# Fifteen small, unused loads queued behind the last weight piece of a decode kernel

## The chip, the cores and the metric

The kernel runs on one core of a Trainium2 chip. The metric is the device time of one execution in microseconds (us). Before the change the median of three runs is 1329.7 us, with 1329.65 the lowest and 1329.88 the highest. A core has a matrix engine (PE), a vector engine (DVE), a scalar engine (ACT), GpSimd (POOL) and SyncE (SP, which only issues transfers and handles semaphores). Each engine follows its own instruction list, and engines wait for each other by semaphores. Sixteen DMA engines move data between the chip's memory (HBM) and the core's on-chip memory (SBUF). A transfer is issued by one engine's instruction list, is cut into packets over the DMA engines, and raises a semaphore when it has landed.

## The reference

One decode step for two batch rows `x` of 1024 elements: a gated mix of cached attention (A) and a small gated-MLP mixer (B).

```python
g = _sigmoid((x * gate_w).sum(-1, keepdims=True))
# A: q = x @ wq, 32 heads of 128, cache of 16384 positions for each batch and head
scores = einsum("bhqd,bhkd->bhqk", q, k_cache) * (Dh ** -0.5)
a = einsum("bhqk,bhkd->bhqd", softmax(scores), v_cache) -> (B, 1, H*Dh) @ wo
# B: (shifts with a sequence of 1 leave zeros, so gelu(layernorm(x) @ w1) meets w2 as zero)
h  = _gelu(_layernorm(x) @ w1);  x1 = x + shifted(h) @ w2
b  = x1 + _gelu(_layernorm(x1) @ w3) @ w4
return g * a + (1 - g) * b
```

All tensors are bfloat16. The two caches hold 2 x 32 x 16384 x 128 elements each, 537 MB together, and they are read once.

## The kernel before

The 32 heads are worked in 16 pairs, and each pair has two batch rows, so there are 32 units. A unit needs one K tile and one V tile. Each is 128 partitions by 64 KB and is loaded by one transfer from SP (`load_k`, line 113, `load_v`, line 118). For a K tile DVE transposes it in pieces (line 435) and PE forms the scores (line 441), then comes the softmax (lines 459 to 489), and PE multiplies the probabilities with the V tile (`pv`, line 495). A hardware loop (`tc.For_i`, line 684) does a pair in each round, one odd and one even unit. In its last round a conditional block (`tc.If`, line 688) also does the last unit, `last_unit`.

All instructions are kept in the order in which they are written on each engine (`in_order`, line 668), so the written order is the order of each queue.

The end of the kernel, which the change touches, runs like this:

- `last_unit` issues seven weight pieces from SP, the list `TAIL` (line 550), through `load_tail` (line 565): all of `wo`, then `w4` in three pieces of 16, 9 and 3 rows per partition, then the remaining 5 rows of `w1` in three pieces of 2, 2 and 1. Each piece has a semaphore of its own, `tail0` to `tail6`. The first two go out as `pv(0)` frees their place, the other five after `pv(1)`. All seven stand in SP's hardware queue (q1 in the profile) in that order. `w1`'s last piece is 128 partitions by 2048 bytes.
- Behind `last_unit` the loop ends. There all engines meet in a barrier: each finishes what it has, signals, and goes on when POOL has seen all of them. In the profile this is at lines 684 and 724.
- Then `output` (line 643) turns the attention result (`turn_heads`, line 526), and PE adds the weight pieces one by one, each behind a wait on the piece's semaphore (line 652). Behind the last `w4` piece `write_out` (line 578) gathers the two result rows and stores them by one transfer from ACT on queue q10 (line 586), which raises the semaphore `stored`. Behind the last `w1` piece ACT applies a GELU to the hidden row (line 663). That row meets only zeros in the reference, but the kernel computes it.
- POOL writes a one-element tile `end_mark` (line 664) and waits for `stored` (line 666). That is POOL's last work before the barrier that ends the program, in which again all engines meet: each engine drains and signals, POOL collects the signals and lets them go.

At the start of the kernel there are three small transfers on SP's queue that the prediction uses: `x` (two rows of 2048 bytes, line 101) and `gate_w` (one row of 2048 bytes, line 102), between the first `w1` piece (line 98) and `wq` (line 91).

Of the kernel before, what the change touches and what calls it, by code (L numbers as in the profile page):

```python
# [11 lines left out]
BF16 = mybir.dt.bfloat16  # L12
# [11 lines left out]
def kernel(  # L24
# [15 lines left out]
    nc = tc.nc  # L40
    P = nc.NUM_PARTITIONS
# [24 lines left out]
    const = ctx.enter_context(tc.tile_pool(name="const", bufs=1))  # L66
# [7 lines left out]
    def misc_psum(shape, dtype=FP32):  # L74
        return mps.tile(shape, dtype, tag="misc", name="misc")
# [41 lines left out]
    def load_v(hp, b, cell=V_CELL):  # L117
        nc.sync.dma_start(out=region(cell, NJ * Dh), in_=cache_rows(A_v_cache, hp, b))
# [6 lines left out]
        out=ident_s[:], in0=ident_f[:], scalar1=-scale, scalar2=None, op0=ALU.mult  # L125
# [10 lines left out]
        out=mask4[:], in_=mask4[:], compare_op=ALU.is_ge, fill=0.0,  # L136
# [3 lines left out]
        out=mask4[:], in_=mask4[:], compare_op=ALU.is_ge, fill=0.0,  # L140
# [11 lines left out]
        out=lmat[:].rearrange("p (g h k) -> p g h k", h=2, k=4),  # L152
        in_=hm2[:].unsqueeze(1).unsqueeze(3).to_broadcast([P, P // 8, 2, 4]),
# [5 lines left out]
        out=lane[:],  # L159
        in_=ident_f[:].rearrange("p (c k) -> p k c", k=QP),  # L160
# [5 lines left out]
    for g in range(Q4):  # L166
        nc.vector.tensor_scalar(
            out=spread[:, g],
# [159 lines left out]
    for shift in (1, -1, 2, -2):  # L328
# [10 lines left out]
        out=x1_rows[:], in_=oacc[1][:, 0:G1], func=ACTF.Copy, scale=omg_row[:, 0:1]  # L339
# [21 lines left out]
    for k in range(2):  # L361
        wide = mlp.tile([P, 16, QP], FP32, tag="wide", name="wide")
        nc.scalar.activation(  # L363
            out=wide[:].rearrange("p (c e) i -> p c e i", e=2),
            in_=oacc[k][:].rearrange("p (c i e) -> p c e i", i=QP, e=2),
# [15 lines left out]
    for e in range(2):  # L381
        half = slice(e * HALF, (e + 1) * HALF)
        nc.vector.tensor_copy(
            out=qdu[half].rearrange("p u v -> p (u v)"),
            in_=qdps[half, e].rearrange("p k g n -> p (k g n)"),
# [27 lines left out]
    def begin_rows(into, saved):  # L413
        for g in range(Q4):
            nc.tensor.matmul(
                into[g][QP * g : QP * g + B, 0:G1],
                lhsT=ident_f[:, QP * g : QP * g + B],
                rhs=saved[:],
                start=True,
                stop=False,  # L420
                skip_group_check=True,
            )
# [29 lines left out]
    def score_first(hp, b):  # L452
        write_qw(hp, b)
        score_chunks(b, halves[1 - b], True, False)

    def score_second(b):
        score_chunks(b, halves[b], False, True)

    def softmax_a(b):
        S = S_tiles[b]  # L460
        st = ppool.tile([P, GT, QP], FP32, name="St")
        nc.vector.transpose(out=st[:].rearrange("p j r -> p (j r)"), in_=S[:])  # L462
        m = stat.tile([P, 1], FP32, name="m")
        nc.vector.tensor_reduce(out=m[:], in_=st[:, :, 0:NG], axis=AX.XY, op=ALU.max)  # L464
        Dm = ppool.tile([P, P], FP32, name="Dm")
        nc.scalar.activation(out=Dm[:], in_=ident_s[:], func=ACTF.Copy, scale=m[:, 0:1])  # L466
        st_tiles[b] = (st, Dm)

    def softmax_b(b):
        st, Dm = st_tiles.pop(b)  # L470
        R_ps = misc_psum([P, P])
        nc.tensor.matmul(R_ps[:], lhsT=ones_f[:], rhs=Dm[:], start=True, stop=True)  # L472
        nb = stat.tile([P, 1], FP32, name="nb")
        rs = stat.tile([P, 1], FP32, name="rs")
        parts = [slice(e * HALF, (e + 1) * HALF) for e in range(2)]
        for rows in parts:
            nc.vector.tensor_reduce(out=nb[rows], in_=R_ps[rows, rows], axis=AX.X, op=ALU.min)  # L477
        for e, rows in enumerate(parts):
            nc.scalar.activation(  # L479
                out=pts[b][rows, :, e, :].rearrange("p (m a) k -> p a k m", a=GT // 4),  # L480
                in_=st[rows, :, 0:NG].rearrange("p (a k) m -> p a k m", k=4),
                func=ACTF.Exp,
                bias=nb[rows],
                scale=scale,
                accum_out=rs[rows],
            )
        tot_ps = misc_psum([P, 1])
        nc.tensor.matmul(tot_ps[:], lhsT=lmat[:], rhs=rs[:], start=True, stop=True)  # L488
        nc.vector.reciprocal(out=rinvs[b][:], in_=tot_ps[:])  # L489

    def pv(b, cell=V_CELL):
        V = view(cell)
        for g in range(NJ // 4):
            q = g % Q4
            nc.tensor.matmul(  # L495
                oacc[b][QP * q : QP * q + 8, :],
                lhsT=pts[b][:, g].rearrange("p h k -> p (h k)"),
                rhs=V[:, 4 * g : 4 * g + 4, :].rearrange("p j d -> p (j d)"),
                start=(g < Q4),
                stop=(g >= NJ // 4 - Q4),  # L500
            )
# [4 lines left out]
    def pv_end(hp, b):  # L506
        osb = ppool.tile([P, 4 * Dh], FP32, name="osb")
        nc.scalar.activation(  # L508
            out=osb[:], in_=oacc[b][:], func=ACTF.Copy, scale=rinvs[b][:, 0:1]
        )  # L510
        ot = misc_psum([P, 2])
        for k in range(4):
            nc.tensor.matmul(  # L513
                ot[:], lhsT=osb[:, k * Dh : (k + 1) * Dh], rhs=lane[:, k : k + 5 : 4],
                start=(k == 0), stop=(k == 3),
            )
        nc.vector.tensor_scalar(  # L517
            out=o_all[:, b, bass.ds(2 * hp, 2)], in0=ot[:], scalar1=g_rep[:, b : b + 1],
            scalar2=None, op0=ALU.mult,
        )  # L520
# [5 lines left out]
    def turn_heads():  # L526
        apart = mlp.tile([P, B, H, Q4], BF16, name="apart")
        for b in range(B):
            nc.vector.tensor_tensor(
                out=apart[:, b],  # L530
                in0=o_all[:, b].unsqueeze(2).to_broadcast([P, H, Q4]),
                in1=mask4[:].unsqueeze(1).to_broadcast([P, H, Q4]),
                op=ALU.mult,
            )
        ps = misc_psum([P, B, QP])
        for b in range(B):
            nc.tensor.matmul(
                ps[:, b], lhsT=apart[:, b].rearrange("p h c -> p (h c)"), rhs=lane_b[:],
                start=True, stop=True,
            )  # L540
        t = mlp.tile([P, QP, B], BF16, name="o_turned")
        nc.vector.tensor_copy(out=t[:], in_=ps[:].rearrange("p b r -> p r b"))
        return t
# [17 lines left out]
    def tail_piece(k):  # L561
        group, cell, at, src, r, n = TAIL[k]
        return region(cell, n * D, at * D)

    def load_tail(k):
        group, cell, at, src, r, n = TAIL[k]
        dma = nc.sync.dma_start(out=tail_piece(k), in_=src[:, r * D : (r + n) * D])
        dma.then_inc(tail_sems[k], 16)
        tc.no_tile_sem_insts.add(dma.ins.name)
        tc.add_to_no_dep_group(group, dma.ins)  # L570


    end_mark = const.tile([1, 1], FP32, name="end_mark")
    stored = tc.alloc_semaphore("stored")
    out_row = mlp.tile([B, D], BF16, name="out_row")
# [51 lines left out]
    def last_unit(hp):  # L627
        V_LAST = 0
        score_first(hp, 1)
        load_v(hp, 1, V_LAST)  # L630
        score_second(1)
        softmax_a(1)
        pv(0)
        load_tail(0)
        load_tail(1)
        pv_end(hp, 0)
        softmax_b(1)
        pv(1, V_LAST)
        for k in range(2, len(TAIL)):
            load_tail(k)  # L640
        pv_end(hp, 1)

    def output():
        begin_rows(arows, x1_rows)
        o_turned = turn_heads()
        hidden = [oacc[0]] * Q4
        begin_rows(hidden, h_early)
        nc.scalar.activation(
            out=h_rows[0:1, 0:1], in_=o_turned[0:1, 0, 0:1], func=ACTF.Gelu_apprx_tanh
        )  # L650
        for k, (group, cell, at, src, r, n) in enumerate(TAIL):
            nc.tensor.wait_ge(tail_sems[k], 16)
            if src is wo_rows:
                add_rows(arows, o_turned, 0, tail_piece(k), False, group)
            elif src is w4_rows:
                mm = add_rows(arows, h2T, r, tail_piece(k), r + n == FC, group)
                if r + n == FC:
                    tc.declare_fence(mm.ins, group=group)
                    write_out()
            else:  # L660
                mm = add_rows(hidden, xn1T, r, tail_piece(k), r + n == KC, group)
                tc.declare_fence(mm.ins, group=group)
        nc.scalar.activation(out=h_rows[:], in_=oacc[0][:, 0:G1], func=ACTF.Gelu_apprx_tanh)  # L663
        mark = nc.gpsimd.memset(end_mark[:], 0.0)
        tc.declare_fence(mark.ins, group="stored")
        nc.gpsimd.wait_ge(stored, 16)

    def in_order():

# [59 lines left out]
```

## Time and profile before

| what | value |
|---|---|
| median of three runs | 1329.7 us |
| time of the profiled execution | 1329.7 us |
| its span, first to last instruction | 1327.7 us |
| TensorE clock granted, share of full speed | 0.782 |
| HBM rate over the span | 431 GB/s |
| busy: PE, DVE, ACT, POOL | 760.3, 647.6, 132.5, 12.1 us |
| packets on q1 (SP), q10 (ACT) | 10662, 148 |
| share of time of the 16 DMA engines: q1, q10 | 99.4%, 0.4% |

The time is 2.0 us longer than the span: what lies before the first and behind the last instruction. The DMA engines are busy for nearly the whole span, so the kernel as a whole goes at the rate of its loads. What happens once the last load has landed is a stretch of about 1.7 us by the last rows of the timeline, and it consists of PE's last matmuls, ACT's GELU, and the barrier.

Beside what each engine did, the trace records every DMA packet (start, duration, bytes, queue) and every increment of a semaphore (its time). A transfer's own increments come as 4-byte packets behind its data packets. A packet's record does not name its DMA engine, but on one DMA engine the next packet's record starts 3 to 4 ns before the end of the one in front, so that neighbours can be matched over a short stretch.

### The profile page before, as it was taken

Reading aid. Unit: us, or ns where it says so; the run is one execution under the profiler, and the core shown is the slowest. Engines: PE = TensorE matmul, PEld = TensorE weight load, DVE = VectorE, ACT = ScalarE, POOL = GpSimd, SP = SyncE. Lnnn points to the kernel's source line nnn. Section 1 sums busy time; section 2 is a strip of 40 time slices with the busy share of each in tenths; the row PEclk is TensorE's granted clock in tenths of the full one; section 3 lists DMA queues with packets and bytes.
Section 4 is the critical chain, followed back from the end, with each engine's and each line's share of the span. In section 5 each row is a group of like instructions: output and inputs, shape, how many; then the busy total and the mean of one; then the engine's idle time right before and its main releaser. Section 6 shows DMA issues by size and latency. Waiting matters only on the chain.

```text
span 1327.7 us, 12974 instructions
## 1 busy us (share of the span) xinstructions
PE 760.3 (57%) x4956; PEld 330.6 (25%) x4956; DVE 647.6 (49%) x507; ACT 132.5 (10%) x207; POOL 12.1 (1%) x48
## 2 busy tenths in 40 slices
PE   3465566655556665555666555566655556665554
PEld 1122222222222222222222222222222223222222
DVE  2554455554445555444555544455554445555420
ACT  0011110011111001111100111110011111101110
POOL 1000000000000000000000000000000000000000
PEclk9677888777788877778887777888777788877776
DMA  9999999999999999999999999999999999999998
GB/s 403 441 439 423 435 434 438 424 432 440 438 426 432 440 423 434 438 440 424 432 440 434 428 434 438 424 434 438 440 424 432 440 424 432 438 440 424 432 440 369
DMA packets 10820, 572.69 MB, mean 431 GB/s; under 512 B 1205, under 2 KB 1205, under 8 KB 1850
## 3 DMA queue, kind: packets, MB, share of 16 engines
q1 hardware_dynamic: 10662, 570.44, 99.4%
q10 hardware_dynamic: 148, 2.10, 0.4%
q8 instruction: 8, 0.13, 0.0%
q14 instruction: 2, 0.02, 0.0%
HBM read 572.53 MB, written 0.00 MB: 431 GB/s over the span
## 4 chain that ended last, share of the span: by engine, by line
DMA 61%; PE 11%; DVE 10%; issue 4%; ACT 0%; DVEq 0%; PEld 0%; SPq 0%; ACTq 0%
DMA mem<-in_A_k_cache_dram 59%; PE S L441 11%; DVE KT L435 10%; DMA mem<-in_B_w_dram 3%; PE oacc L495 0%; DVEq L435 0%; ACT pt L479 0%; PEld L495 0%; SPq L113 0%; PE misc L513 0%; PE oacc L402 0%; ACT osb L508 0%; PEld misc L488 0%; ACT h_rows L663 0%; PE misc L472 0%
## 5 line engine op out<-in xcount | busy, mean ns | idle before, releaser
L441 PE MATMUL S<-KT,qw 128*128 128x512 bf16 x2048 | 548.2, 418 | 363.2 <-DVE KT L435 362.8
L435 DVE STREAM_TRANSPOSE KT<-mem 128x2048 f32<-128x2048 f32 x256 | 570.7, 2282 | 270.9 <-DMA mem<-in_A_k_cache_dram 212.0
L441 PEld LDWEIGHTS <-qw 128*128 128x128 bf16 x2048 | 216.5, 106 | 686.8 <-issue 482.6
L495 PE MATMUL oacc<-mem,pt 128*8 128x512 bf16 x2048 | 118.2, 384 | 7.6 <-DMA mem<-in_A_v_cache_dram 7.6
L466 ACT ACTIVATE Dm<-ident_s,m 128x128 f32<-128x128 f32 x32 | 12.9, 402 | 978.5 <-PE oacc L495 941.4
L479 ACT ACTIVATE pt<-St,nb 64x256 bf16<-64x256 f32 x64 | 89.7, 1401 | 61.1 <-DVE nb L477 60.2
L517 DVE TENSOR_SCALAR o_all<-misc,g_rep 128x2 f32 (+1 forms) x32 | 7.0, 220 | 163.2 <-PE misc L513 163.2
L488 PE MATMUL misc<-rs,lmat 128*128 128x1 f32 x64 | 18.7, 362 | 107.9 <-ACT pt L479 61.3
L495 PEld LDWEIGHTS <-pt 128*8 128x8 bf16 x2048 | 47.3, 87 | 75.6 <-issue 23.8
L513 PE MATMUL misc<-lane,osb 128*128 128x2 f32 x256 | 33.4, 252 | 45.3 <-ACT osb L508 45.3
L489 DVE RECIPROCAL rinv<-misc 128x1 f32<-128x1 f32 x32 | 5.4, 169 | 108.5 <-PE misc L488 60.5
L462 DVE STREAM_TRANSPOSE St<-S 128x512 f32<-128x512 f32 x32 | 22.9, 717 | 66.4 <-PE L495 64.4
L513 PEld LDWEIGHTS misc<-lane,osb 128*128 128x128 f32 x256 | 31.1, 191 | 61.0 <-ACT osb L508 31.6
L488 PEld LDWEIGHTS misc<-rs,lmat 128*128 128x128 f32 x64 | 16.0, 311 | 114.8 <-ACT pt L479 65.3
L508 ACT ACTIVATE osb<-oacc,rinv 128x512 f32<-128x512 f32 x32 | 22.0, 687 | 88.3 <-PE oacc L495 88.3
L479 ACT ACTIVATION_READ_ACCUMULATOR pt<-St,nb 64x1 f32 x64 | 30.6, 477 | 0.0
L389 POOL TENSOR_TENSOR qw<-qdu,mask 128x16 bf16<-128x16 bf16 x32 | 7.3, 261 | 1161.6 <-PEq L688 1074.6
L477 DVE TENSOR_REDUCE nb<-misc 64x1 f32<-64x64 f32 x64 | 14.2, 222 | 7.0 <-PE misc L472 4.9
L472 PE MATMUL misc<-Dm,ones_f 128*128 128x128 f32 x64 | 16.6, 346 | 0.0
L464 DVE TENSOR_REDUCE m<-St 128x1 f32<-128x256 f32 x32 | 13.4, 420 | 1.1
L583 DVE CAST out_row<-arow 2x256 bf16<-2x256 f32 x1 | 0.4, 413 | 26.9 <-PE S L402 26.9
L217 DVE STREAM_TRANSPOSE turn<-wide 128x512 f32<-128x512 f32 (+2 forms) x4 | 3.0, 744 | 17.5 <-ACT wide L363 11.5
(104 smaller groups left out, 95.4 us busy)
## 6 DMA issues: line engine op xcount, KB each, us to landing
mem<-in_B_w_dram SPq DMA_DIRECT2D x1, 7168.0 KB, 31.6
mem<-in_B_w_dram SPq DMA_DIRECT2D x1, 4096.0 KB, 42.1
mem<-in_B_w_dram SPq DMA_DIRECT2D x1, 2304.0 KB, 32.2
mem<-in_B_w_dram ACTq DMA_DIRECT2D x1, 2048.0 KB, 11.8
mem<-in_B_w_dram SPq DMA_DIRECT2D x2, 768.0 KB, 21.1
mem<-in_B_w_dram SPq DMA_DIRECT2D x2, 512.0 KB, 33.9
mem<-in_A_k_cache_dram SPq DMA_DIRECT2D x32, 27.8
mem<-in_A_v_cache_dram SPq DMA_DIRECT2D x32, 32.4
```

Of the source, the lines that this page charges most:

```text
L435: nc.vector.transpose(out=kt[:], in_=Kc.rearrange("p j d -> p (j d)").bitcast(FP32))
L441: nc.tensor.matmul(S, lhsT=qw[b][:, v, NG - 1 - m : NG - 1 - m + P], rhs=ktb[:, half * GT : (half + 1) * GT, w, :, e], start=(first and n ...
L462: nc.vector.transpose(out=st[:].rearrange("p j r -> p (j r)"), in_=S[:])
L464: nc.vector.tensor_reduce(out=m[:], in_=st[:, :, 0:NG], axis=AX.XY, op=ALU.max)
L466: nc.scalar.activation(out=Dm[:], in_=ident_s[:], func=ACTF.Copy, scale=m[:, 0:1])
L472: nc.tensor.matmul(R_ps[:], lhsT=ones_f[:], rhs=Dm[:], start=True, stop=True)
L477: nc.vector.tensor_reduce(out=nb[rows], in_=R_ps[rows, rows], axis=AX.X, op=ALU.min)
L479: nc.scalar.activation(out=pts[b][rows, :, e, :].rearrange("p (m a) k -> p a k m", a=GT // 4), in_=st[rows, :, 0:NG].rearrange("p (a k) m ...
L488: nc.tensor.matmul(tot_ps[:], lhsT=lmat[:], rhs=rs[:], start=True, stop=True)
L495: nc.tensor.matmul(oacc[b][QP * q : QP * q + 8, :], lhsT=pts[b][:, g].rearrange("p h k -> p (h k)"), rhs=V[:, 4 * g : 4 * g + 4, :].rearra ...
L508: nc.scalar.activation(out=osb[:], in_=oacc[b][:], func=ACTF.Copy, scale=rinvs[b][:, 0:1])
L513: nc.tensor.matmul(ot[:], lhsT=osb[:, k * Dh : (k + 1) * Dh], rhs=lane[:, k : k + 5 : 4], start=(k == 0), stop=(k == 3),)
```

## The change

A tile `marks` of 16 partitions by 512 elements is added that nothing reads, and a semaphore `marked`. Behind the seven weight pieces, still in `last_unit`, SP issues fifteen transfers, number k from 1 to 15. Number k copies k rows of 8 x k bytes out of `wo` (from the first k of its 128 row groups, which lie 64 KB apart) to k partitions of `marks`. They write disjoint columns. All of them raise `marked`, by 16 each. At the end POOL waits for `marked` to reach 240 behind its wait for `stored`.

```diff
+    marks = const.tile([16, 512], BF16, name="marks")
+    marked = tc.alloc_semaphore("marked")
+    wo_flat = A_wo.rearrange("(p r) n -> p (r n)", p=P)
+    MARKS = range(1, 16)
+
+    def load_marks():
+        at = 0
+        for k in MARKS:
+            dma = nc.sync.dma_start(
+                out=marks[0:k, at : at + 4 * k], in_=wo_flat[0:k, 0 : 4 * k]
+            )
+            dma.then_inc(marked, 16)
+            tc.no_tile_sem_insts.add(dma.ins.name)
+            tc.add_to_no_dep_group("marked", dma.ins)
+            at += 4 * k
...
         for k in range(2, len(TAIL)):
             load_tail(k)
+        load_marks()
         pv_end(hp, 1)
...
         mark = nc.gpsimd.memset(end_mark[:], 0.0)
         tc.declare_fence(mark.ins, group="stored")
+        tc.declare_fence(mark.ins, group="marked")
         nc.gpsimd.wait_ge(stored, 16)
+        nc.gpsimd.wait_ge(marked, 16 * len(MARKS))
```

## The prediction

> **What bounds the kernel now.** I read the page first: its chain of work, then the waits of SP's queue, then the timeline of the last 55 us, and last the trace's records of packets and semaphore increments at both ends of the span. The page says that the loads bound the whole:
>
> ```profile
> PEclk9677888777788877778887777888777788877776
> DMA  9999999999999999999999999999999999999998
> ...
> DMA 61%; PE 11%; DVE 10%; issue 4%; ACT 0%; DVEq 0%; PEld 0%; SPq 0%; ACTq 0%
> ```
>
> The reader is to see that the DMA row is full in every slice. A transfer that stands in front of other loads costs its own time. The fifteen new ones stand behind all other loads of SP's queue, so what counts is who waits for them. First SP, which must issue them before the barrier at the loop's end; its waits near the end, in us (total, times, longest):
>
> ```profile
> SPq L724 <- DVE out_row L583: 28.6, 1, 28.6
> ...
> SPq L724 <- ACT h_rows L663: 2.2, 1, 2.2
> SPq L684 <- DVE o_all L517: 2.0, 1, 2.0
> ```
>
> SP arrives at the loop's end 2.0 us before DVE, and afterwards it stands for 28.6 and 2.2 us. Next the timeline (start, duration, what, and in brackets the idle time before it):
>
> ```profile
> 1288.85 3.10 SPq L567 DMA_DIRECT2D mem<-in_B_w_dram  x5
> ```
>
> ```profile
> 1295.84 0.09 POOL L664 MEMSET end_mark<- 1x1 f32 x1 [103.23 <-POOLq L724]
> ...
> 1297.13 0.20 ACT L648 ACTIVATE h_rows<-o_turned 1x1 bf16<-1x1 bf16 x1
> ...
> 1305.93 0.38 PE L402 MATMUL arow<-mem,o_turned 128*2 128x256 bf16 x2 [8.75 <-DMA mem<-in_A_wo_dram]
> ...
> 1324.71 0.53 ACTq L586 DMA_DIRECT2D out_dram<-out_row  x1
> 1325.43 0.10 PEld L402 LDWEIGHTS <-xn1T 128*2 128x2 bf16 x8 [1.12 <-DMA mem<-in_B_w_dram]
> 1325.43 1.01 PE L402 MATMUL oacc<-mem,xn1T 128*2 128x256 bf16 x12 [0.62 <-DMA mem<-in_B_w_dram]
> ...
> 1326.49 0.38 ACT L663 ACTIVATE h_rows<-oacc 128x256 bf16<-128x256 f32 x1 [1.92 <-PE oacc L402]
> ```
>
> SP's last issue is over at 1291.95. The barrier lets the engines go at 1295.8. The preparation of the output takes 1.5 us, and then PE stands 8.75 us until `wo` is there. At the end PE's last matmuls follow w1's last piece, whose increments arrive up to 1326.02, ACT is done at 1326.87, and SP's signal at 1327.02 is the last that POOL collects, at 1327.04. From there 0.71 us remain. So the present end goes w1, PE, ACT, SP, barrier. POOL is early: `stored` is full at 1325.96, POOL's drain is over at 1326.19, and it stands 0.85 us.
>
> **The change part by part.**
>
> *Issues on SP.* Fifteen instructions. The nearest rows are the small loads at the start:
>
> ```profile
> 1.25 0.33 SPq L101 DMA_DIRECT2D rows<-in_A_x_dram  x1
> ...
> 1.63 0.22 SPq L102 DMA_DIRECT2D rows<-in_gate_w_dram  x1
> ```
>
> With the 0.53 us of the store as the other end and some 0.045 us between two, fifteen take 4.0 to 8.6 us, near 5.5 us by the row with two rows. SP leaves them at 1296.0 to 1300.6. Its remaining steps to the barrier took 0.75 us before the wait and 0.5 us behind it, so the barrier opens at 1297.2 to 1301.9 where it opened at 1295.8. DVE, PE, ACT and POOL all wait for it. What they do there is 1.5 us of preparation in front of PE's 8.75 us wait for `wo`: the delay of 1.5 to 6.1 us is covered and costs nothing; the cover is gone at about 0.73 us for each issue. What is late next would be wo's matmuls, with further waits of 3.34 and 2.33 us behind them.
>
> *The data.* In all 8 x (1 + 4 + ... + 225) = 9920 bytes, at most 960 on one DMA engine, which by the 80 ns from one 2048-byte packet to the next is 0.04 us. They are behind w1 in the same queue, so w1, PE and ACT lose nothing. The result's two rows go by q10 and share DMA engines with them; see below.
>
> *The increments.* This is where I expect the cost. At the start x (two rows) made two data packets and two increments, and gate_w (one row) one of each. I read from that that k rows use k DMA engines (if they used fewer, the first would still get all fifteen). The gate packet began 6 ns behind the second increment packet of x, on the same DMA engine, so small transfers share their first engine: it gets fifteen increments, the next fourteen, and so on. On that engine three increments went out back to back: that of w2 (q10), of x and of gate_w, packets at 9.492, 9.498 and 9.584 us. They landed at 9.887, 10.069 and 10.251: 0.182 us apart each time, though the packets were 0.006 and 0.086 us apart. On x's other engine the pair landed at 9.742 and 9.924, again 0.182. So increments of one DMA engine take turns, also over two queues, and 2048 bytes of data between two of them add nothing. (Where they lie farther apart, as in w1's pieces, an increment lands some 0.44 us after its packet.)
>
> The sixteen increments of w1's last piece land between 1324.23 and 1326.02, nine of them from 1325.69 on. Which engine is the first of the small ones isn't recorded; only the store's two packets, at 1325.48 and 1325.52 on idle engines, say that its two engines were through w1 by then. An engine late in w1 among the first three gives 1325.85 plus 13 to 15 times 0.182, that is 1328.2 to 1328.6. Taking every order of the sixteen as equally likely (the first two done by 1325.92), the mean of the latest is 1328.3 and eight in ten lie between 1328.0 and 1328.6. The store's own increments join the same line on two of these engines, at most 0.18 more. I take 1328.4 for the last of `stored` and `marked`.
>
> *POOL.* It waits for `marked` with nothing behind but the drain and the final barrier, for which all engines wait. Increments that land by 1325.96 + 0.85 = 1326.81 would cost nothing. 1328.4 is 1.6 us later, which moves the end from the chain w1, PE, ACT, SP to the chain w1, increments, POOL. The second wait instruction is some tens of ns. One semaphore more and fifteen instructions more in a block that runs once I cost at nothing: in the loop SP waits 16 us at a time for DVE (509.5 us over 31 waits).
>
> *Bounds of a turn.* Nothing in the trace shows fifteen in a row, or packets of 8 to 120 bytes. Below: turns that overlap, 0. Above: each transfer begins only when the one before has landed, 0.44 us after its packet plus some 0.06, so 0.5 us; then the same average puts the last landing at 1332.8, +6.0 us. I take 0.182, since the three rows agree to the ns with and without data between.
>
> *The sum.* 0 (issues) + 0 (data) + 1.6 (increments and POOL) on a profiled execution of 1329.7 us, which is also the median: 1331.3 us, +0.12%. From no change this kernel's measurement tells about 0.2%, here 2.7 us.
>
> [...]
>
> **The rivals.**
>
> *A costlier turn (slower).* Place: the first DMA engine's line behind w1. Price: more than 0.182 us for each transfer. From 0.26 us on, the last landing is past 1329.5 and the kernel is over 0.2% slower. For it: 8-byte pieces have no row here, the trace has only three pairs, and each transfer's read could wait for the former's increment. Against it: x and gate_w, with separate transfers and data between. [...]
>
> *SP is held up (slower).* SP had at most seven transfers outstanding (at 1291.95), each issue still at 0.33 to 0.37 us. With 22 the queue might be full. SP would then issue the last ones only when w4 and w1 have drained, near 1322 to 1326, and the barrier and all of the output come behind: 1.4 us preparation, then PE's 6.3, 3.2, 1.6 and 0.8 us, then the store, about 2.2. That ends 12 to 15 us later: 1342 to 1345. No row speaks for it, none shows more than seven.
>
> *All hidden (same).* If increments overlap, `marked` is full by 1326.8, and the end stays with ACT: 1329.7. The 0.182 us speaks against it.
>
> *Faster.* Only a different spread of the last loads over the engines could do it; SP's order in front of the marks is unchanged. I see no row for more than some tenths.
>
> **How the numbers follow.** Turns of about 0.18 us, 1330.9 to 1332.3: 0.46. All hidden: 0.06. Costlier turn: 0.35. SP held up: 0.10. Faster: 0.03. Same is 0.46 + 0.06 = 0.52, slower 0.45, faster 0.03. The likeliest case alone says 1331.3. For eight in ten I leave out SP held up and the turns beyond 0.5 us (some 0.10), and start where all is hidden: 1329.6 to 1336.0.
>
> **What would show it.** After: SP's fifteen issues of 0.22 to 0.53 us from 1292 on; the barrier at 1297 to 1302 and PE's wait for `wo` shorter by the same, its wo matmuls still at about 1305.9; w1, PE and ACT at the end as before; the increments of `marked` on the fullest engine 0.18 us apart, the last near 1328.4; and a span of 1329.3. Wrong it would be by a turn that is not 0.18 us, by an SP issue that lasts microseconds, or by wo matmuls that begin late.

## The result, and the profile after

The changed kernel takes 1333.55 us in the median of eight runs (1332.29 to 1334.89). The kernel before takes 1329.82 in the eight runs beside it (1329.49 to 1329.97). The ratio is 1.003, with a 95% interval of 1.0019 to 1.0041: slower by 3.7 us, or 0.28%. The time lies in the predicted range (1329.6 to 1336.0), but it isn't the forecast of 1331.3, and it lies past the 0.2% that the prediction took as the line between slower and no change (the interval reaches down to 0.19%). The runs also spread over 2.6 us, where the kernel before spreads over 0.5.

The profiled execution took 1333.65 us, with a span of 1331.6. The waits of SP's queue and of the engines near the end, in the columns used before (total, times, longest, in us):

```profile
SPq L743 <- DVE out_row L599: 12.8, 1, 12.8
...
SPq L743 <- ACT h_rows L680: 1.0, 1, 1.0
```

```profile
PE S L415 <- PEq L743: 21.5, 1, 21.5
...
DVE out_row L599 <- PE S L402: 10.6, 1, 10.6
```

SP's 2.0 us wait for DVE at the loop's end is gone, and its long wait of 28.6 us has shrunk to 12.8. PE, on the other hand, stands 21.5 us at the barrier. The timeline says why (start, duration, what, idle time before it):

```profile
1292.05 22.84 SPq L581 DMA_DIRECT2D marks<-in_A_wo_dram  x15
...
1316.34 0.09 POOL L681 MEMSET end_mark<- 1x1 f32 x1 [124.38 <-POOLq L743]
...
1317.88 0.14 PEld L402 LDWEIGHTS <-o_turned 128*2 128x2 bf16 x4 [0.28 <-DVE o_turned L542]
...
1322.39 1.84 PEld L402 LDWEIGHTS <-o_turned 128*2 128x2 bf16 x71 [2.13 <-issue]
1324.24 1.61 PEld L402 LDWEIGHTS <-h2T 128*2 128x2 bf16 x57
1326.68 1.40 PEld L402 LDWEIGHTS <-h2T 128*2 128x2 bf16 x55 [0.82 <-issue]
1328.09 0.53 PEld L402 LDWEIGHTS <-xn1T 128*2 128x2 bf16 x20
...
1329.35 0.53 ACTq L602 DMA_DIRECT2D out_dram<-out_row  x1
1329.93 0.38 ACT L680 ACTIVATE h_rows<-oacc 128x256 bf16<-128x256 f32 x1 [0.72 <-DVE out_row L599]
```

The fifteen issues last 22.84 us, not 4.0 to 8.6. The first five take 0.24 to 0.29 us each. The sixth takes 2.61, the seventh 4.80, and the rest 1.18 to 2.38 each. So SP is done with its issues 22.9 us later, at 1314.89. It no longer waits for DVE, and the barrier opens 20.5 us later, at 1316.26 instead of 1295.76. By then `wo` has long landed. PE does all of its output work in one go, from 1317.88 on, and no row of it waits for a transfer any more: the two waits that are left inside it say "issue". The store goes out at 1329.35, 4.64 us later than before. POOL had 0.85 us to spare, and the difference, 3.8, is what the span grew by (from 1327.75 to 1331.59).

The increments did what was predicted of them: the last one for `marked` landed at 1328.04. But `stored` was full only at 1330.60, so they cost nothing here.

Before, the end of the kernel hung on the chain w1, PE, ACT, SP. Now it hangs on SP's issues, the barrier, PE, the store and POOL.

### The profile page after: what moved, and what is told of

It reads as the page before. It is cut to its first block, busy times and chain, and to the rows that moved or that the text cites. A ratio compares the mean times of both kernels' runs of the same rounds, so it can differ in the third digit from the quotient of the medians.

```text
span 1331.6 us, 12990 instructions
## 1 busy us (share of the span) xinstructions
PE 754.6 (57%) x4956; PEld 329.5 (25%) x4956; DVE 648.1 (49%) x507; ACT 132.5 (10%) x207; POOL 12.0 (1%) x48
## 5 line engine op out<-in xcount | busy, mean ns | idle before, releaser
L462 DVE STREAM_TRANSPOSE St<-S 128x512 f32<-128x512 f32 x32 | 22.9, 717 | 66.4 <-PE L495 64.4
L415 PE MATMUL S<-x_rows,ident_f 128*2 128x256 f32 x4 | 1.0, 608 | 21.5 <-PEq L743 21.5
L472 PEld LDWEIGHTS misc<-Dm,ones_f 128*128 128x128 f32 x64 | 11.0, 216 | 0.4 <-issue 0.4
## 6 DMA issues: line engine op xcount, KB each, us to landing
mem<-in_B_w_dram SPq DMA_DIRECT2D x2, 768.0 KB, 21.5
```

## The experiments

The theory after this reading: SP is held in its issues because too much stands in its queue, and the price is the late barrier. Rivals: the small transfers or their increments cost the time where they are.

### The transfers issued behind the barrier

```diff
         for k in range(2, len(TAIL)):
             load_tail(k)
-        load_marks()
         pv_end(hp, 1)
...
         o_turned = turn_heads()
+        nc.vector.memset(marks[:], 0.0)
+        load_marks()
```

> The fifteen transfers are issued behind the loop's barrier (at the start of the output, behind a memset of their tile), with everything else as in the changed kernel. Theory: SP held in its issues costs only because SP owes the barrier its signal; here it owes nobody anything until 1324, so the barrier opens near 1295.8 again, PE works through the pieces as they land, and only the increments are left: marked full near 1328.0 to 1328.6, 1330.9 to 1331.4 us, about 1.5 above the kernel before. Rival, the increments cost nothing (other work covers them): 1329.7. Rival, the transfers cost the 3.7 us by themselves wherever they are issued: 1333.5.

It took 1331.12 us (1330.84 to 1331.44), against 1329.88 (1329.55 to 1330.11) for the kernel before in these runs: ratio 1.001, interval 1.0000 to 1.0019. The interval reaches down to no change, but none of the ten runs overlaps with any of the 27. Its timeline:

```profile
1296.33 0.09 POOL L682 MEMSET end_mark<- 1x1 f32 x1 [103.17 <-POOLq L744]
...
1298.11 16.80 SPq L581 DMA_DIRECT2D marks<-in_A_wo_dram  x15
1306.14 4.63 PEld L402 LDWEIGHTS <-o_turned 128*2 128x2 bf16 x128 [8.55 <-issue]
...
1324.94 0.53 ACTq L602 DMA_DIRECT2D out_dram<-out_row  x1
...
1326.76 0.38 ACT L681 ACTIVATE h_rows<-oacc 128x256 bf16<-128x256 f32 x1 [1.96 <-PE oacc L402]
```

SP is held here too, 16.80 us for the fifteen, but it owes nobody a signal. The barrier is early, PE starts on `wo` when it lands, and the store goes out at 1324.94. The trace's semaphore records have the last increment of `marked` at 1328.00 and POOL going on at 1328.02, 0.74 us after the last of the other engines. So this kernel has the end that the prediction described, and its 1.24 us stand beside the predicted 1.6.

### A late barrier without the transfers

```diff
         for k in range(2, len(TAIL)):
             load_tail(k)
+        nc.sync.wait_ge(tail_sems[1], 16)
         pv_end(hp, 1)
```

> The kernel before, without any of the fifteen transfers, but SP waits for the landing of w4's first piece (near 1315.3) ahead of the loop's barrier. Theory (the late barrier is the cost): the barrier opens near 1316.2 as in the changed kernel, and the time is 1333.5 with a spread of some 2 us between runs. Rival (the small transfers or their increments are the cost): 1329.7.

It took 1334.22 us (1333.64 to 1334.68), ratio 1.0032, interval 1.0019 to 1.0044. The barrier opened at 1317.44, 1.2 us later than in the changed kernel:

```profile
1317.52 0.09 POOL L665 MEMSET end_mark<- 1x1 f32 x1 [124.96 <-POOLq L725]
...
1323.80 1.84 PEld L402 LDWEIGHTS <-o_turned 128*2 128x2 bf16 x71 [1.92 <-issue]
...
1329.96 0.53 ACTq L586 DMA_DIRECT2D out_dram<-out_row  x1
```

Not one small transfer is in this kernel, and it loses 4.3 us, with the same kind of stop inside PE's work. So a late barrier alone is enough for a loss of this size. The spread of 1 us is less than the 2 expected.

The second form of this edit waits for `tail_sems[0]`, that is for `wo`:

> The kernel before, but SP waits for the landing of wo (near 1305.8) ahead of the loop's barrier. Theory: the barrier opens near 1306.7, PE is ready near 1308.2, 2.3 us behind wo's landing, and its later waits for w4 (3.3 and 2.3 us) take that up: 1329.7 to 1330.0. Rival (any delay of the barrier beyond PE's 8.75 us wait is paid in full): 1332.

1329.89 us (1329.66 to 1330.23), ratio 1.0001, interval 0.9991 to 1.001. The barrier opened near 1307.5 and PE's output work began at 1309.15, 3.2 us later than before. Its later waits took that up, as the prediction said of delays beyond the 8.75 us. PE stopped for "issue" here too, for 1.86 and 2.54 us, and still came to a wait for weights behind that, so the stops cost nothing here.

### Five transfers instead of fifteen

```diff
-    MARKS = range(1, 16)
+    MARKS = range(1, 6)
```

> Only the transfers of 1 to 5 rows, in the place of the change. Theory (SP is held from the sixth on, since its queue is full): five issues of 0.24 to 0.29 us, the barrier near 1295.8 to 1296, marked full by 1326.9 at the latest, 1329.7 to 1329.9. Rival (each small transfer costs a fifteenth of the 3.7 us): 1331.0.

1329.95 us (1329.70 to 1330.21), ratio 1.0001, interval 0.9991 to 1.001. Five issues of 0.24 to 0.29 us, barrier at 1295.6. Five cost nothing that these runs can tell, so the loss is no fixed price for each transfer. At which number between five and fifteen it sets in, no run shows.

### The same fifteen on ACT's queue

```diff
-        load_marks()
         pv_end(hp, 1)
+        load_marks()
...
-            dma = nc.sync.dma_start(
+            dma = nc.scalar.dma_start(
                 out=marks[0:k, at : at + 4 * k], in_=wo_flat[0:k, 0 : 4 * k]
```

> The same fifteen transfers, issued by ACT behind its last activation of the loop (near 1293.8), so on queue q10, which is empty then; the rest as in the changed kernel. Theory (SP's own queue is full, and that holds SP): ACT isn't held, fifteen issues of 0.25 to 0.55 us are over by 1298 to 1302, the barrier opens by 1303, within PE's wait for wo, and the transfers land long before the end, among the loads: 1329.7 to 1330.0. Rival (what is full is shared by both queues): ACT is held instead of SP, the barrier opens near 1316, 1333.5.

1329.85 us (1329.77 to 1330.25), ratio 1.0002, interval 0.9992 to 1.0011. Each issue took 0.24 to 0.50 us, at the same time at which SP would have been held, and the barrier opened at 1299.6:

```profile
1293.23 5.54 ACTq L581 DMA_DIRECT2D marks<-in_A_wo_dram  x15
```

So what holds SP belongs to SP's queue, and is not something that both queues share. The same 9920 bytes and 120 increments cost nothing when they don't stand behind the last weights.

### What fills the queue

Four kernels ask whether packets or transfers count, and on what. Each was run once. The first replaces the fifteen by one transfer of 16 rows with 30 pieces of 8 bytes each:

```diff
-        for k in MARKS:
-            dma = nc.sync.dma_start(
-                out=marks[0:k, at : at + 4 * k], in_=wo_flat[0:k, 0 : 4 * k]
-            )
+        dma = nc.sync.dma_start(
+            out=marks[:, 0 : 30 * 8].rearrange("p (j e) -> p j e", e=8)[:, :, 0:4],
+            in_=wo_flat[0:16, 0 : 30 * 8].rearrange("p (j e) -> p j e", e=8)[:, :, 0:4],
+        )
```

> One transfer in the place of the fifteen: 16 rows, each of 30 pieces of 8 bytes, so that each DMA engine gets 30 data packets and one increment, as many packets as the fullest engine has in the change, but one transfer and one turn. If packets for each DMA engine fill the queue: this single issue lasts some 20 us, the barrier opens at 1313 to 1316, and the time is near 1333. If the number of transfers outstanding fills it (twelve went out freely): one issue of 0.3 us, barrier at 1295.8, 1329.7.

It took 1330.03 us beside 1329.67. Its issue took 0.42 us. Taken alone this speaks for transfers and against packets.

The second gives all fifteen one row:

```diff
-                out=marks[0:k, at : at + 4 * k], in_=wo_flat[0:k, 0 : 4 * k]
+                out=marks[0:1, at : at + 4 * k], in_=wo_flat[0:1, 0 : 4 * k]
```

> Fifteen transfers in the place of the change, each of one row (8 to 120 bytes), so all on one DMA engine: 15 data packets and 15 increments there, none on the others. If what fills is counted for each DMA engine or in transfers: SP is held as in the change, from about the sixth on, barrier near 1316, 1333.5. If it is the sum over the engines (240 packets in the change, 30 here): no hold, barrier near 1297, and only the turns are left, 1330.5 to 1331.4.

It took 1333.23 us beside 1329.67. SP's row in the timeline:

```profile
1292.08 22.85 SPq L581 DMA_DIRECT2D marks<-in_A_wo_dram  x15
```

22.85 us against 22.84 in the change, and the sixth is again the first to be held. One DMA engine's share is enough; the sum over the engines (30 packets instead of 240) isn't what counts. In this run the fifteen increments stand alone on their engine, and the trace has them landing from 1324.669 to 1327.214 us, each 0.18 us behind the one before (2.545 us over 14 steps, single steps of 0.180 to 0.186): the predicted turn, with packets of 8 to 120 bytes.

The third joins w1's last three pieces, which takes two transfers and 18 packets for each engine out of the queue:

```diff
-        ("hidden0", 1, 0, w1_rows, W1_EARLY, 2),
-        ("hidden1", 1, 2, w1_rows, W1_EARLY + 2, 2),
-        ("hidden2", 1, 4, w1_rows, W1_EARLY + 4, 1),
+        ("hidden0", 1, 0, w1_rows, W1_EARLY, 5),
```

> The changed kernel with the three last pieces of w1 as one transfer of five rows, so two transfers and 18 packets for each DMA engine fewer stand ahead of the small ones. If the number of transfers is what SP's queue can take (twelve went out freely, the thirteenth was held): the first seven small ones go out freely and the eighth is held. If it is packets for each DMA engine: some nine more, so nearly all fifteen go out freely. If neither counts but only the time or the data ahead: the sixth is held as before. The time is of no use here, since PE gets w1 later.

```profile
1288.90 2.42 SPq L565 DMA_DIRECT2D mem<-in_B_w_dram  x3
1291.38 5.27 SPq L579 DMA_DIRECT2D marks<-in_A_wo_dram  x15
```

All fifteen go out freely in 5.27 us, so with twenty transfers outstanding, where the change was held at the thirteenth. That rules out a limit on transfers and fits packets for each DMA engine. (The time, 1330.89 us beside 1329.58, can't be set against the others, since PE gets w1 later here.) It then clashes with the single transfer of 30 pieces, unless an issue is handed over without its packets having room, and the next issue pays. The fourth kernel puts three transfers of one row behind that one:

```diff
+        for k in range(3):
+            at = 240 + 4 * k
+            dma = nc.sync.dma_start(
+                out=marks[0:1, at : at + 4], in_=wo_flat[0:1, at : at + 4]
+            )
```

> The one transfer of 16 rows with 30 pieces each, whose own issue was not held, and behind it three transfers of one row. If the packets that stand ahead on a DMA engine decide (some 70 by the change, where the sixth was held): the 31 packets of the big one bring that count to about 90, and one of the three is held for many us, until some 20 packets are gone, near 1310 or later; the barrier then opens 15 to 20 us late. If a transfer's packets don't count once it is handed over, or it is transfers that count: none is held, barrier near 1296, 1329.7 to 1330.2.

```profile
1292.02 0.43 SPq L579 DMA_DIRECT2D marks<-in_A_wo_dram  x1
1292.50 25.02 SPq L588 DMA_DIRECT2D marks<-in_A_wo_dram  x3
1319.38 1.28 ACT L671 ACT_TABLE_LOAD   x1 [25.82 <-PEq L749]
```

It took 1337.66 us beside 1329.80. The first of the three, one row of 8 bytes, holds SP for 22.5 us. The big transfer's packets do count, for the issue behind it. The time is 4 us above the change's: the barrier opened 3.0 us later, at 1319.28, and PE's clock after it was lower, as told below.

How many is only roughly known. When the change's sixth transfer was held, at 1293.63, a DMA engine had by its packets in the trace five of wo's left and wo's increment, nine for each of the other six weight pieces, and ten for the five small ones: 70. The sixth and seventh went through, at 1296.24 and 1301.08, as one group of engines finished a packet, with 68 in front. With w1 in one piece the fifteenth went out freely with 68 or 69 in front. Some 70 fits these. It doesn't fit all: the eighth followed after 1.2 us, in which that group finished nothing, and the first of the three above went through with more than 70 by the same count. What exactly is counted stays open.

### The increments doubled

The fifteen twice, behind the barrier:

```diff
-    MARKS = range(1, 16)
+    MARKS = [*range(1, 16)] * 2
```

> The fifteen transfers twice, behind the barrier, as in marks_behind_barrier (1331.12). Theory of the turns (0.18 us for each increment on one DMA engine): fifteen more increments on the first engine, 2.7 us more, marked full near 1330.7, 1333.6 to 1334.0. Rival (the 1.2 us there is a fixed price of waiting for a second semaphore, or of anything behind w1): 1331.1 to 1331.4.

1333.26 us (1333.01 to 1333.45), ratio 1.0026, interval 1.0016 to 1.0036; 2.14 us more than with fifteen. `marked` was full at 1330.29 instead of 1328.00. `stored`, whose two increments stand in the same lines, was full a turn later still, at 1330.47, and was the last thing POOL waited for. So the 1.24 us is no fixed price of a second wait: it grows with the number of increments. It grew by 0.14 to 0.15 us for each added transfer, not 0.18. The likely reason is that with fifteen the last increment came on another engine than the first, one with fewer of them that was later through w1. The records fit this: with fifteen, the seven landings in a row that end with the last one stand 0.20 us apart, and with thirty the last eight stand 0.18 us apart. But the trace doesn't name the engines, so it isn't shown.

## Why the prediction was right or wrong, point by point

**Issues on SP: wrong, and this is the step that failed.** "Fifteen take 4.0 to 8.6 us" came from two transfers at the start of the kernel, with little in the queue. Here some 60 packets stood ahead on a DMA engine when the first went out, by the count used above, and SP's issues lasted 22.84 us. The cover was named rightly (PE's 8.75 us and its later waits). A barrier 11.7 us late was still free (the wait for `wo`), so the 8.75 us that are gone at 0.73 us for each issue are not all of it. The measured mean of an issue is 1.5 us, and with the barrier 20.5 us late all of the cover is used up.

**The range held the time by luck.** Its upper end came from the costlier turn, which didn't happen, and SP held up, which did, was left out of it. The time fell inside because this rival cost less than a third of what it was said to.

**SP is held up, the rival with a chance of 0.10: it happened, at a smaller price.** It was said to end at 1342 to 1345. Its barrier at 1322 to 1326 was too late: SP is let go at 1314.89, beside w4's first piece, whose last increment came at 1315.54, not after w1. And PE's durations were taken from rows in which PE had a reduced clock (0.67 to 0.79 of full in the stretches up to 1321). In the profiled execution of the change it had 0.96, and the matmuls of `wo` and `w4` took 7.5 us instead of 11.9, or 10.1 with the stops told below. Nor is the higher clock sure: in the kernel with one transfer of 30 pieces and three behind it, where PE also did this work in one go, the clock over it was 0.65, and the same matmuls took 10.1 us without the stop. "No row speaks for it, none shows more than seven" was true, and it was a reason for a larger chance than 0.10, since nothing in the trace bounded what eight to 22 would do.

**Data: right.** w1's last piece landed at 1326.10 in the changed kernel and at 1326.02 before.

**Increments and POOL: right in mechanism and nearly in size, but hidden in the change itself.** Predicted were turns of 0.182 us and a last landing between 1328.0 and 1328.6. The last landing came at 1328.04. Turns of 0.18 us stand where fifteen increments are alone on their engine; in the change the last six landings of the row that ends at 1328.04 stand 0.20 us apart. So 0.182, which three rows agreed on to the ns, isn't the same for all, and what it depends on stays open. In the change the late PE covers the increments. Where the barrier is early, 1.24 us are measured for the predicted 1.6. (Of w1's last sixteen increments eight land from 1325.69 on, not nine; the estimate of 1328.3 doesn't hang on it.)

**A costlier turn, the rival with a chance of 0.35: it fell.** Fifteen on one engine landed within 2.55 us, 0.180 to 0.186 us apart, and the turns read in the change stand 0.20 us apart. No run shows a turn of the 0.26 us from which it counted, or of the 0.5 us that the upper end of the range took. The slower result has another cause.

**Code and semaphore at nothing: right for the loop, but a new cost came up behind the barrier.** PE stops with nothing to wait for but "issue", in the chain of work (start, duration, what):

```profile
1320.45 1.94 issue
...
1326.05 0.62 issue
```

Both stops lie on the path to the store. As an estimate from these rows, without them the store would have gone out 2.56 us earlier, at 1326.8, and the span would have grown by some 1.3 us instead of 3.8. So most of the late barrier's price in this execution passes in the stops. Packets of 16384 bytes on the instruction queue begin at 1319.98 and 1323.86; the first is over at 1321.00, 1.4 us before PE goes on. In the kernel before such packets come at 1301.08, 1310.74 and 1320.27, beside waits for weights. I read the stops as waits for PE's next instructions. The other late barriers fit: with SP waiting for w4, for `wo` (two stops), with fifteen of one row and with the three behind 30 pieces, PE goes on 1.4 to 1.5 us after such a packet's end (behind the second packet of the change it is 1.7). But no run took these loads away, so the reading isn't shown. Nor is it shown what makes the runs spread more widely: the stops and the granted clock both change between these kernels (stops of 0.9 to 2.6 us in all where the loss is paid, clocks of 0.65 to 0.96).

## What to carry to other kernels

Here SP's issues took 0.24 to 0.29 us each until some 70 packets stood ahead on a DMA engine, and 1.18 to 4.80 us each from there on. Before adding many small transfers behind large ones, count the packets that stand ahead on a DMA engine and look for who waits for the issuing engine next, here a barrier of all engines, which opened 20.5 us late. Three other places were measured: on ACT's queue the fifteen cost nothing that the runs can tell (1329.85 us); behind the barrier SP was still held, but only 1.24 us of turns remained; behind w1 merged into one piece they went out in 5.27 us, with no time that can be set against the others. And a semaphore raised by many small transfers behind the last load landed in turns: its last increment came 1.9 us behind w1's last piece in the change (1328.04 after 1326.10), and with thirty transfers behind the barrier at 1330.29.

## What was not expected of the hardware

- SP was held in single issues for up to 4.80 us with some 70 packets ahead on a DMA engine, and for 22.5 us by a transfer of 8 bytes with some 90 ahead; ACT's queue took fifteen in 0.24 to 0.50 us each at such a time.
- A transfer of 31 packets for each engine was handed over in 0.42 us (0.43 in the second kernel with it) with some 60 packets ahead; the issue behind it lasted 22.5 us.
- Increments that wait for each other landed some 0.18 us apart (0.180 to 0.186 with fifteen on one engine), also from two queues or with 2048 bytes of data between them (0.182 each time, at the start of the kernel before); at the end of the change and of the fifteen behind the barrier they stand 0.20 us apart.
- PE's clock after a late barrier was 0.96 in one execution and 0.65 in another, and the same 240 matmuls took 7.5 and 10.1 us.
